# Loading the gate rows of a head pair as two broadcasts to 64 partitions each

## The chip, the cores and the metric

The kernel runs on one core of a Trainium2 chip. The metric is the device time of one execution in microseconds (us); the time of a kernel is the median of several runs. A trace of one further execution, taken by the hardware profiler, gives the rows below. The engines are PE (TensorE, matmuls; PEld its weight loads), DVE (VectorE), ACT (ScalarE), POOL (GpSimd) and SP (SyncE, which here only issues DMA transfers, in program order). The DMA transfers themselves run on 16 DMA engines.

## The reference

Three stages run one after the other on 2 x 576 tokens with 512 features:

```python
# attention with a forget gate: B, H, S, D = 2, 8, 576, 64
cum = np.cumsum(np.log(np.clip(f, 0.0001, 1.0)), axis=-1)
scores = q @ k.T / np.sqrt(D) + cum[:, :, :, None] - cum[:, :, None, :]
attn = softmax(where(causal, -1e9, scores));  x = attn @ v        # heads side by side: 1152 x 512
# mixture of 4 experts, 512 -> 1024 -> 512, weighted by p = domain_probs / sum
x = sum(p[:, e:e+1] * (np.maximum(x @ w1[e], 0) @ w2[e]) for e in range(4))
# MLP, 512 -> 2048 -> 512
h = x @ w_in;  out = (h / (1 + np.exp(-1.702 * h))) @ w_out
```

## The kernel before, in words

The tokens are four chunks (`CH`): 256 and 320 tokens of each of the two batch entries. Attention and the expert layers are interleaved: `attention()` is a generator of attention steps, and the main loop over `seq` emits expert matmuls (`emit_l1`, line 687, and `emit_l2`, line 736, twelve matmuls for each of four groups `g`) and pulls attention steps between them. Chunk 0 is done first with its order fixed by hand (`in_turn`, `first_step`). Then two passes over head pairs follow: the pass of chunk 1 (four head pairs), then that of chunks 2 and 3 (four more). Elsewhere a scheduler places the instructions of each engine.

For each head pair the kernel loads keys (`kq`) and queries (`qr`), values (`vd`), and the row of `cum` of each head, written to DRAM as `cumd` before. `load_cum` does the last: into two tiles `cb` (one for each head, the first 512 columns of its row in all 128 partitions) and one tile `cbs` (576 columns; head 0's row in partitions 0 to 63, head 1's in partitions 64 to 127, for the last 64 queries of both heads, which are worked on together). `prep_cum` on POOL adds the causal mask `tri` to the diagonal blocks: lines 404 and 407 for `cb`, line 410 for `cbs`, one small addition for each half of the tile. `emit_max` (line 475, DVE) adds `cb` or `cbs` to the scores in PSUM and takes the row maximum. ACT exponentiates (line 491), POOL normalises (line 500), PE transposes (line 518), ACT copies the result (`ph`, line 56), and PE multiplies with the values (line 548).

Expert weights come in pairs of groups into `wst` (`load_pair`, 512 KB). ACT rounds each group to `whi` (line 56), DVE takes the remainder `wlo` (line 173), and the matmuls of lines 687 and 736 use both.

All these loads are issued through `load` (line 62) on one queue, that of SP, in the order of the program. `cbs_p` has two buffers, so the load of a `cbs` waits until DVE has read the one from two head pairs before; what stands behind it on the queue waits too.

Of the kernel before, what the change touches and what calls it, by code (L numbers as in the profile page):

```python
# [15 lines left out]
B, H, S, D = 2, 8, 576, 64  # L16
# [19 lines left out]
def attn_moe_mlp(ctx: ExitStack, tc: tile.TileContext, qk0, qk1, qk2, v0, vp, fg, dp, wa_moe, wb_moe, wa_mlp, wb_mlp, outT):  # L36
# [8 lines left out]
    def pool(name, bufs, space=None, scope=ctx):  # L45
        kw = {} if space is None else {"space": space}
        return scope.enter_context(tc.tile_pool(name=name, bufs=bufs, **kw))
# [12 lines left out]
    def load(out, in_):  # L60

        ins = nc.sync.dma_start(out=out, in_=in_)
        if start[0]:
            tc.keep_in_program_order(ins)
# [37 lines left out]
    cumd = pool("cumd", 1, bass.MemoryType.DRAM).tile([16, S], F32, name="cumd")  # L102
# [284 lines left out]
    def load_cum(p, h0):  # L387

        cs, b, s0 = p
        st = pairs[p, h0]  # L390
        r = b * H + h0
        st["cb"] = [cb_p.tile([128, 896], F32, tag="cb", name="cb") for _ in range(2)]
        for g, cb in enumerate(st["cb"]):
            load(cb[:, :512], cumd[r + g:r + g + 1, :512].to_broadcast([128, 512]))
        st["cbs"] = cbs_p.tile([128, S], F32, tag="cbs", name="cbs")
        load(st["cbs"], cumd[r:r + 2, :].unsqueeze(1).to_broadcast([2, 64, S]))

    def prep_cum(p, h0):

# [185 lines left out]
    def first_step(i):  # L585
# [30 lines left out]
        if i == 0:  # L616
            load_cum(p, h0)
# [5 lines left out]
    def attention():  # L623
# [16 lines left out]
        for i in range(len(seq) + L_X2 + 1):  # L640
# [9 lines left out]
            for k in [k for k in nxt if first[k] == i + 2]:  # L650
                load_cum(*k)
# [281 lines left out]
```

## Time and profile before

| | |
|---|---|
| time, median of 3 runs | 744.79 us (743.59 to 745.51) |
| profiled execution | 746.29 us, of which 744.6 us from the first to the last instruction (the span) |
| busy in the span | PE 716.6, PEld 686.9, DVE 460.5, POOL 289.4, ACT 272.3 us |
| mean granted clock of TensorE | 0.982 of full speed |

An engine's busy time is a sum over stages. Matmuls are pipelined and their ends are modelled, so a busy PE is not a PE at its peak; where PE stands idle or runs at a lower granted clock is read from the trace by stage.

### The profile page before, as it was taken

What the parts mean: (1) busy time and instruction counts of PE and PEld (TensorE: products, weight loads), DVE (VectorE), ACT (ScalarE), POOL (GpSimd) and SP (SyncE); (2) the same over time, 40 slices, a digit from 0 to 9 for tenths busy, and PEclk for the clock granted to TensorE, in tenths of its full rate; (3) what the DMA queues carried; (4) which work ended last, traced back from release to release, by engine and by line L of the source; (5) the groups of instructions that cost most, each with busy time, mean ns of one, the idle gap of its engine ahead of it and who ended that gap; (6) DMA issues with size and microseconds to landing.
All of it is one profiled execution on the core that took longest, in us unless ns stands there. A gap on an engine that the chain in (4) does not pass through costs nothing.

```text
span 744.6 us, 12024 instructions
## 1 busy us (share of the span) xinstructions
PE 716.6 (96%) x4520; PEld 686.9 (92%) x4520; DVE 460.5 (62%) x1023; ACT 272.3 (37%) x636; POOL 289.4 (39%) x368
## 2 busy tenths in 40 slices
PE   7986888999999999999999999999999999999998
PEld 4676777888999999999999999999999999999998
DVE  6474357667667999999999833334983124424422
ACT  5444447656642232232212211222444433323420
POOL 4585577887242204223323333232352222222220
PEclk9698999999999999999999999999999999999999
DMA  8484544624215554644443401000100000000012
GB/s 241 139 269 126 173 139 151 208 90 119 86 57 192 157 181 142 183 150 128 142 142 96 105 27 57 1 1 1 57 1 0 1 1 1 1 1 0 1 44 85
DMA packets 31226, 68.83 MB, mean 92 GB/s; under 512 B 3224, under 2 KB 4768, under 8 KB 31168
## 3 DMA queue, kind: packets, MB, share of 16 engines
q1 hardware_dynamic: 31128, 68.02, 29.4%
q8 instruction: 36, 0.59, 0.3%
q14 instruction: 22, 0.18, 0.1%
q10 hardware_dynamic: 40, 0.04, 0.0%
HBM read 65.62 MB, written 2.41 MB: 91 GB/s over the span
## 4 chain that ended last, share of the span: by engine, by line
PE 76%; DVE 9%; DMA 7%; POOL 2%; issue 2%; ACT 2%; SPq 1%; POOLq 0%; ACTq 0%; DVEq 0%
PE m L736 34%; PE m L687 33%; PE x L548 3%; DMA wst<-in_wb_moe_dram 3%; DMA wst<-in_wa_moe_dram 3%; PE s L449 3%; PE t L518 3%; DVE wlo L173 2%; POOL e L500 1%; ACT e L491 1%; DVE hl L719 1%; DVE wf L228 1%; DVE cvd L234 1%; DVE tmp L750 1%; DVE cvt L222 1%
## 5 line engine op out<-in xcount | busy, mean ns | idle before, releaser
L752 POOL TENSOR_TENSOR acc<-acc,tmp 128x384 f32<-128x384 f32 (+3 forms) x112 | 111.9, 1009 | 240.1 <-DVE tmp L750 238.5
L687 PE MATMUL m<-xh,whi 128*128 128x384 f32 (+2 forms) x624 | 126.4, 322 | 11.9 <-ACT whi L56 5.5
L736 PE MATMUL m<-hh,wlo 128*128 128x384 f32 (+2 forms) x640 | 128.1, 319 | 1.3 <-DVE wlo L173 1.3
L736 PE MATMUL m<-hh,whi 128*128 128x384 f32 (+2 forms) x640 | 128.7, 320 | 0.6 <-DVE hl L714 0.5
L736 PE MATMUL m<-hl,whi 128*128 128x384 f32 (+2 forms) x640 | 127.4, 319 | 0.0
L687 PE MATMUL m<-xl,whi 128*128 128x384 f32 (+2 forms) x624 | 126.4, 322 | 0.0
L687 PE MATMUL m<-xh,wlo 128*128 128x384 f32 (+2 forms) x624 | 126.2, 322 | 0.0
L173 DVE TENSOR_TENSOR wlo<-wst,whi 128x512 fp32r<-128x512 f32 x112 | 96.3, 862 | 42.8 <-ACT whi L56 40.5
L56 ACT ACTIVATE whi<-wst 128x512 fp32r<-128x512 f32 x108 | 67.1, 628 | 138.2 <-PE m L687 62.8
L687 PEld LDWEIGHTS m<-xh,whi 128*128 128x128 f32 x624 | 104.0, 189 | 12.9 <-ACT whi L56 5.7
L736 PEld LDWEIGHTS m<-hh,wlo 128*128 128x128 f32 x640 | 106.0, 188 | 2.1 <-DVE wlo L173 1.9
L736 PEld LDWEIGHTS m<-hh,whi 128*128 128x128 f32 x640 | 106.2, 189 | 1.5 <-DVE hl L714 0.7
L736 PEld LDWEIGHTS m<-hl,whi 128*128 128x128 f32 x640 | 106.0, 189 | 0.2
L687 PEld LDWEIGHTS m<-xl,whi 128*128 128x128 f32 x624 | 104.8, 190 | 0.3
L687 PEld LDWEIGHTS m<-xh,wlo 128*128 128x128 f32 x624 | 104.6, 190 | 0.3
L727 POOL TENSOR_TENSOR hl<-tmp,hh 128x384 fp32r<-128x384 f32 x48 | 49.0, 1024 | 133.3 <-ACT hh L56 133.2
L718 ACT ACTIVATE hh<-m 128x384 fp32r<-128x384 f32 (+2 forms) x108 | 47.3, 439 | 114.4 <-PE m L687 114.4
L719 DVE SCALAR_TENSOR_TENSOR hl<-m,hh 128x384 fp32r<-128x384 f32 (+2 forms) x108 | 53.0, 494 | 33.9 <-ACT hh L718 33.8
L725 DVE TENSOR_TENSOR tmp<-m,sg 128x384 f32<-128x384 f32 x48 | 26.6, 554 | 54.2 <-ACT sg L724 54.2
L750 DVE TENSOR_TENSOR tmp<-m,dpb 128x384 f32<-128x384 f32 (+2 forms) x80 | 40.8, 511 | 30.3 <-PE m L736 27.3
L500 POOL TENSOR_SCALAR e<-e,sm 128x128 f32<-128x128 f32 (+4 forms) x72 | 44.9, 634 | 36.1 <-DVE sm L498 28.6
L491 ACT ACTIVATE e<-e,mx 128x128 f32<-128x128 f32 (+4 forms) x72 | 42.0, 583 | 29.0 <-DVE mx L475 27.5
(99 smaller groups left out, 783.3 us busy)
## 6 DMA issues: line engine op xcount, KB each, us to landing
wst<-in_wa_moe_dram SPq DMA_DIRECT2D x28, 512.0 KB, 4.2
wst<-in_wb_moe_dram SPq DMA_DIRECT2D x28, 512.0 KB, 4.4
mst<-in_wa_mlp_dram SPq DMA_DIRECT2D x16, 512.0 KB, 3.8
mst<-in_wb_mlp_dram SPq DMA_DIRECT2D x16, 512.0 KB, 3.6
cb<-cumd SPq DMA_DIRECT2D x16, 256.0 KB, 4.8
qr<-in_qk_dram SPq DMA_DIRECT2D x12, 256.0 KB, 10.7
kq<-in_qk_dram SPq DMA_DIRECT2D x8, 352.0 KB
vd<-in_vp_dram SPq DMA_DIRECT2D x8, 320.0 KB, 10.6
```

The source lines that it names most:

```text
L56: return nc.scalar.activation(out=out, in_=in_, func=AF.Copy)
L173: nc.vector.tensor_sub(lf, raw, f(hf))
L491: nc.scalar.activation(out=e[:, off:off + w], in_=e[:, off:off + w], func=AF.Exp, scale=-1.0, bias=mx, accum_out=sm[:, 0, k:k + 1])
L500: nc.gpsimd.tensor_scalar(out=e[:, off:off + w], in0=e[:, off:off + w], scalar1=sm[:, 0, i:i + 1], scalar2=1.0, op0=ALU.mult, op1=ALU.mult)
L687: nc.tensor.matmul(p[:, :n], lhsT=w[:, k, :], rhs=x[c][:, k, :], start=(j == 0 and k == 0), stop=(j == 2 and k == 3))
L718: nc.scalar.activation(out=hh[:, g, :n], in_=p[:, :n], func=AF.Relu)
L719: nc.vector.scalar_tensor_tensor(out=hl[:, g, :n], in0=p[:, :n], scalar=0.0, in1=f(hh[:, g, :n]), op0=ALU.max, op1=ALU.subtract)
L725: nc.vector.tensor_mul(t[:, :n], p[:, :n], s[:, :n])
L727: nc.gpsimd.tensor_sub(hl[:, g, :n], t[:, :n], f(hh[:, g, :n]))
L736: nc.tensor.matmul(p[:, :n], lhsT=w[:, k, :], rhs=x[:, k, :n], start=(j == 0 and k == 0), stop=(j == 2 and k == 3))
L750: nc.vector.tensor_mul(t[:, :n], p[:, :n], d)
L752: nc.gpsimd.tensor_add(a, a, t[:, z])
```

## The change

```diff
@@ load_cum
         st["cbs"] = cbs_p.tile([128, S], F32, tag="cbs", name="cbs")
-        load(st["cbs"], cumd[r:r + 2, :].unsqueeze(1).to_broadcast([2, 64, S]))
+        for g in range(2):
+            load(st["cbs"][64 * g:64 * g + 64], cumd[r + g:r + g + 1, :].to_broadcast([64, S]))
```

One transfer whose source is walked as two rows, each repeated 64 times, becomes two transfers, each of one row repeated 64 times. The bytes that are written are the same, 288 KB for a head pair, and there are eight head pairs. Line numbers above 396 are one higher in the changed kernel.

On SP's queue, in the pass of chunk 1 around the third head pair, the piece of the difference reads (names are tiles and inputs, `wst` the expert weights):

```order
 L62 DMA wst<-in_wa_moe_dram 128x2x512
 L62 DMA cb<-cumd 128x512 x2
-L62 DMA cbs<-cumd 128x1x576
+L62 DMA cbs<-cumd 64x576 x2
 L62 DMA wst<-in_wa_moe_dram 128x2x512
 L62 DMA vd<-in_vp_dram 128x640
```

Nothing else moves on this queue; at each of the eight places two transfers stand for one, ahead of the same followers.

On POOL, at the same head pair, the kernel before has (`e` are the attention weights, `khi` and `klo` the split keys of a later pair):

```order
L404 TENSOR_TENSOR cb<-cb,tri 128x128
L407 TENSOR_TENSOR cb<-cb,tri 128x128
L53 TENSOR_SCALAR khi<-kq 128x704
L500 TENSOR_SCALAR e<-e,sm 128x576
L410 TENSOR_TENSOR cbs<-cbs,tri 64x64 x2
L374 TENSOR_TENSOR klo<-kq,khi 128x704
L466 MEMSET e 128x64
L500 TENSOR_SCALAR e<-e,sm 128x384 x2
```

and the changed kernel has:

```order
L405 TENSOR_TENSOR cb<-cb,tri 128x128
L408 TENSOR_TENSOR cb<-cb,tri 128x128
L53 TENSOR_SCALAR khi<-kq 128x704
L411 TENSOR_TENSOR cbs<-cbs,tri 64x64
L501 TENSOR_SCALAR e<-e,sm 128x576
L411 TENSOR_TENSOR cbs<-cbs,tri 64x64
L374 TENSOR_TENSOR klo<-kq,khi 128x704
L501 TENSOR_SCALAR e<-e,sm 128x384 x2
L467 MEMSET e 128x64
```

The addition to the first half of `cbs` now stands ahead of the normalisation of `e`, that to the second half behind it. PE, DVE and ACT keep their instructions up to swaps of neighbours in the two passes, and nothing moves behind the attention.

## Rows read from the trace of the kernel before

**Rows 1.** The chain that ended last, its largest shares by line.

```profile
PE m L736 34%; PE m L687 33%; PE x L548 3%; DMA wst<-in_wb_moe_dram 3%; DMA wst<-in_wa_moe_dram 3%; PE s L449 3%; PE t L518 3%; DVE wlo L173 2%; POOL e L500 1%; ACT e L491 1%; DVE hl L719 1%; DVE wf L228 1%; DVE cvd L234 1%; DVE tmp L750 1%; DVE cvt L222 1%
```

**Rows 2.** Busy time by stretch: the pass of chunk 1, then of chunks 2 and 3.

```profile
core 0: us, PE busy (x) PEld busy (x) DVE busy (x) ACT busy (x) POOL busy (x), PEclk, DMA share, GB/s
40.00:120.00 80.00, 62.35 (x430) 55.47 (x429) 45.28 (x128) 37.81 (x99) 55.30 (x87) 0.91 0.51 153
120.00:216.00 96.00, 95.07 (x700) 86.26 (x698) 67.24 (x218) 62.05 (x170) 65.64 (x97) 1.00 0.43 130
```

**Rows 3.** The chain between 38 and 130 us: start, us, what.

```profile
40.48 12.62 DMA wst<-in_wb_moe_dram
...
60.96 10.27 DMA wst<-in_wa_moe_dram
...
101.04 10.12 DMA wst<-in_wb_moe_dram
```

**Rows 4.** PE in order of time, where it stood over 2 us [idle before].

```profile
55.08 0.74 PE L687 MATMUL m<-xh,whi 128*128 128x256 f32 x4 [2.04 <-DVE acc L747]
...
72.00 1.22 PE L687 MATMUL m<-xh,whi 128*128 128x256 f32 x4 [5.48 <-ACT whi L56]
...
94.67 3.96 PE L548 MATMUL x<-ph,vd 128*64 128x320 f32 x20 [4.28 <-ACT ph L56]
...
114.19 0.74 PE L687 MATMUL m<-xh,whi 128*128 128x256 f32 x4 [4.36 <-DVE hl L719]
```

**Rows 5.** SP's queue in order of time at the third head pair.

```profile
60.37 0.51 SPq L62 DMA_DIRECT2D cbs<-cumd  x1
60.96 0.42 SPq L62 DMA_DIRECT2D wst<-in_wa_moe_dram  x1
```

**Rows 6.** Busy time by stretch around two of the four stalls (columns as in rows 2).

```profile
62.00:64.00 2.00, 2.00 (x16) 1.86 (x15) 1.16 (x6) 0.87 (x4) 2.00 (x4) 1.00 0.90 162
64.00:66.00 2.00, 2.00 (x17) 1.86 (x16) 0.00 (x0) 0.00 (x0) 0.26 (x1) 1.00 1.01 336
...
70.00:72.00 2.00, 0.00 (x1) 0.00 (x1) 0.02 (x1) 0.69 (x2) 1.74 (x3) 0.64 0.13 52
72.00:74.00 2.00, 1.44 (x5) 1.15 (x6) 2.00 (x4) 2.00 (x6) 0.66 (x2) 0.50 0.09 35
...
110.00:112.00 2.00, 0.00 (x0) 0.00 (x0) 0.15 (x1) 0.82 (x2) 1.72 (x3) 1.00 0.13 51
```

**Rows 7.** Waits of POOL, 40 to 120 us (us, times, longest), largest.

```profile
POOL cbs L410 <- DMA cbs<-cumd: 15.9, 4, 6.0
```

**Rows 8.** POOL in order of time at the third head pair.

```profile
70.10 0.70 POOL L410 TENSOR_TENSOR cbs<-cbs,tri 64x64 f32<-64x64 f32 x2 [5.85 <-DMA cbs<-cumd]
```

**Rows 9.** DMA issues: count, KB each, median us from issue to landing.

```profile
wst<-in_wa_moe_dram SPq DMA_DIRECT2D x28, 512.0 KB, 4.2
...
dpb<-dpT SPq DMA_DIRECT2D x2, 288.0 KB, 4.4
```

**Rows 10.** A stretch at the start, loads of 64 partitions in flight (columns as rows 2).

```profile
3.00:4.00 1.00, 1.00 (x4) 0.35 (x3) 0.88 (x3) 0.67 (x2) 0.97 (x5) 1.00 0.73 213
```

**Rows 11.** The chain: PE's pieces behind two stalls, and like pieces later.

```profile
73.78 1.09 PE s L449 x3
74.86 1.71 PE m L687 x8
76.57 2.62 PE x L548 x20
...
114.19 2.36 PE m L687 x12
...
116.76 3.00 PE x L548 x20
...
130.82 2.21 PE x L548 x20
...
138.82 0.40 PE s L449 x3
...
229.04 1.44 PE m L687 x12
```

## The prediction, made before the changed kernel ran

> **What bounds the kernel now.** I read the chain that ended last first. Matmuls hold most of it, but two DMA entries stand high in it, the loads of expert weights `wst`, with 3% each [rows 1]. A transfer belongs there only while an engine stands and waits for it, so the next view was busy time by stretch: in the pass of chunk 1, 40 to 120 us, PE is busy for 62.35 of 80 us at a mean clock of 0.91, in the pass after it for 95.07 of 96 us at 1.00 [rows 2]. The loss lies in the first of the two. There the chain runs through four loads of `wst`; three are shown, of 12.62, 10.27 and 10.12 us (the fourth, between the last two, is like them) [rows 3], where the median load of `wst` lands after 4.2 us [rows 9]. PE in order of time shows what that costs: four stalls of 2.04, 5.48, 4.28 and 4.36 us, 16.16 us together, each released by something made from the weights that came late or queued behind it on ACT or DVE [rows 4].
>
> Why are these loads late? On SP's queue the load of `cbs` stands just ahead of `wst`, 60.37 and 60.96 us [rows 5]. `cbs` lands at 70.10 us, 9.7 us after its issue (POOL, which had waited 5.85 us for it, starts then) [rows 8], and `wst` 1.1 us behind it, at 60.96 + 10.27 = 71.23. The load of `dpb`, as large (288 KB, a row repeated over 128 partitions), takes 4.4 us [rows 9]. What differs shows in the share of the DMA engines: from 62 to 66 us it is 0.90 to 1.01, but in the last two microseconds ahead of the landing, 70 to 72, it is 0.13 at 52 GB/s, and at the last stall again 0.13 at 51 GB/s [rows 6]. 0.13 of 16 engines is two engines. So I read the old `cbs` as carried by two engines, 147 KB on each, while the other fourteen go ahead and run dry; `wst` has a share on those two as well, behind `cbs`, and isn't complete before that.
>
> **The change part by part.**
>
> *Issue.* One more transfer for each of eight head pairs, 0.5 us of SP's queue each [rows 5]. Where the queue is waited for, `wst` is issued 0.5 us later; that is in the estimate below. Elsewhere it is hidden by the span of what SP waits for anyway.
>
> *Landing.* No row shows a row broadcast to 64 partitions. The nearest from above is the old load, 9.7 us; from below the broadcast of 288 KB to 128 partitions, 4.4 us. Loads of 64 partitions at the start keep 0.73 of the 16 engines busy [rows 10], so 64 partitions do not confine a transfer to a few. I take about 5 us for both halves, near the lower end.
>
> *The weights behind it.* If the two halves lie evenly on 16 engines, `wst` has 295 KB more ahead of it on all of them: 0.9 us at the 336 GB/s of [rows 6]. I estimate 4.2 + 0.9 us from its issue, which is 0.5 us later: 60.96 + 0.5 + 5.1 = 66.6 in place of 71.23, that is 4.7 us earlier. PE stood from 66.5 (72.00 less 5.48) and restarted 0.8 us behind the landing, so about 0.8 us of this stall stays. At the last stall 101.04 + 5.6 = 106.6 in place of 111.16, 4.5 us earlier against a stall of 4.36; the third is like it. The first, 2.04 us, had its load landing at 53.10; the same two engines hold it, so it goes too. Gain: 16.16 - 0.8 = 15.4 us.
>
> *The clock.* [...] Against like pieces at full clock [rows 11]: behind the second stall 1.09 for 0.40, 1.71 for 0.96 (eight at 1.44 / 12) and 2.62 for 2.21, 1.85 us more; behind the third 3.96 [rows 4] for 2.21, 1.75; behind the fourth 2.36 for 1.44 and 3.00 for 2.21, 1.71. Together 5.3 us, which go where the stalls go. The stall of 2.04 us has no such slow pieces behind it (0.74 for four, not 1.22) [rows 4], so the 0.8 us that stay should cost no clock.
>
> *POOL.* Its waits for `cbs` in the first pass, 15.9 us in four [rows 7], fall to some 3 us: it came to the addition 3.9 us after the issue at the third head pair, so with a landing of 5 to 5.5 us it still waits 1 to 1.5 us, and about as long at the next. This is no further gain but a limit: POOL is busy for 55.30 of the 80 us [rows 2]. PE's stretch would shrink to 80 - 15.4 - 5.3 = 59.3 us. POOL needs 55.3 + 3 = 58.3 if none of its other waits (80 - 55.3 - 15.9 = 8.8 us) remain, and 67 if all do. Both engines would be nearly full, and where they wait for each other time is lost; I take 2 us off.
>
> *Second pass.* PE is idle for 0.93 of its 96 us [rows 2]: 0.8 us is what an earlier `cbs` can bring at most, and I take it. After the attention nothing moves, and what follows starts earlier by as much.
>
> Sum: 15.4 + 5.3 - 2.0 + 0.8 = 19.5 us. The profiled execution took 746.29 us, 1.5 us more than the median shown; 746.3 - 19.5 = 726.8, and for a median 744.8 - 19.5 = 725.3 us.
>
> [...] The trace shows two engines at work at the end of each such burst [rows 6], so the halves are not a mere splitting of one even transfer. [...]
>
> **The rivals.** *POOL sets the pace of the first pass.* If its other waits of 8.8 us stay, the pass takes 67 us and the gain is 13 + 0.8, 731 us. For it: it would then be busy for over 80% of the pass. Against it: in the second pass PE hardly stands with POOL busy for 65.64 of 96, and part of the 8.8 us came behind the late weights.
>
> *The transfers of a burst share the engines without order,* and `wst` is complete only with the last of its burst. In the second burst 2.03 MB are issued together; 0.32 and 0.67 MB have moved by 66 us [rows 6], the rest takes 3.1 us at 336 GB/s, so `wst` would land at 69.1, 2.1 us earlier than now. Four times that is 8.4 us with the clock hardly mended: 736 us. Against it: `cbs` and `wst` landed 1.1 us apart in the order of issue.
>
> *The halves are not spread,* each lands as late as the whole: 744.8 us, within 0.3%, which is about what a measurement of this kernel can tell from no change. [rows 10] speak against it.
>
> *Slower: POOL's new order.* The first half's addition now stands ahead of a normalisation of `e`. If that half landed as late as now, the normalisation would wait up to 5.85 us, and PE's transposes behind it; since PE stood there later anyway, I price it at 2 us, and with 0.5 us of issue ahead of each of four late loads at 4 us: 749 us. It decides only if landing stays near 9 us; under some 5 us POOL hardly waits.
>
> **How the numbers follow.** The forecast as worked out (720 to 730): 0.62. POOL's pace (730 to 735): 0.20. Burst without order: 0.08. Not spread: 0.05. Slower: 0.03. More than 25 us gained: 0.02. The predicted time is the first, 725.3; 720 to 735 holds 0.82. Faster by over 0.3%: 0.62 + 0.20 + 0.08 + 0.02 = 0.92; within: 0.05; slower: 0.03.
>
> **What would show it.** Right: no stretch of the first pass with the DMA share at 0.13; loads of `wst` out of the chain there, or at 4 to 6 us; PE's four stalls gone but for a microsecond, the clock at 1.00 through the pass; POOL's waits for `cbs` at a few microseconds; the span of the first pass near 61 us and all that follows unchanged in length. Wrong: the share of 0.13 still there (not spread); no tail, but `wst` at 8 us (no order); or stalls of PE released by POOL's normalisation (POOL's pace).

## The result, and the profile after

The changed kernel takes 726.04 us (median of 4 runs, 722.93 to 727.28), the kernel before 744.19 us beside it (4 runs, 743.25 to 745.51): ratio 0.9749, 95% interval 0.9719 to 0.9778. In a second comparison on another occasion it was 724.44 against 746.5 us, ratio 0.971 (0.9676 to 0.9743). So the gain is 18 to 22 us. The profiled execution of the changed kernel was its quickest, 722.93 us, and that of before lies 2.1 us above its median; the two traces therefore differ by 23.4 us, more than the medians do.

Where did the time go from? I cut both traces at the same work. The first mark is the first matmul of line 736 (737 after), chunk 0's second expert layer; the second is the end of the third of chunk 1's four products with the values (line 548, 549 after). All four late loads of weights land between them, and this stretch is called the first pass here; the fourth product lies behind the mark, among the work of the second pass. Busy time by stretch, after:

```profile
core 0: us, PE busy (x) PEld busy (x) DVE busy (x) ACT busy (x) POOL busy (x), PEclk, DMA share, GB/s
39.40:99.20 59.80, 56.87 (x428) 50.89 (x429) 45.74 (x128) 37.51 (x96) 55.36 (x84) 1.00 0.58 201
...
99.19:232.96 133.77, 133.77 (x993) 124.94 (x994) 97.32 (x272) 73.20 (x196) 74.53 (x107) 1.00 0.44 140
```

and the same work before ([rows 2] cut it at round numbers):

```profile
40.70:119.80 79.10, 61.52 (x422) 54.84 (x423) 44.84 (x128) 36.95 (x97) 54.46 (x85) 0.91 0.51 152
...
119.76:256.13 136.37, 135.44 (x999) 125.62 (x1000) 97.11 (x272) 73.61 (x196) 75.05 (x106) 1.00 0.45 138
```

The first pass is 19.3 us shorter; the second, cut at the start of a block of 48 matmuls behind the attention (the third mark), 2.6. Of these 21.9 us, 15.6 are idle time of PE (17.58 + 0.93 before, 2.93 + 0 after), and 6.3 are busy time (196.96 against 190.64), at a clock of 1.00 in place of 0.91 in the first pass. The next 1.3 us lie ahead of the first mark (39.4 for 40.7); they are put down to the execution and not to the change, since a kernel that has the old loads up to there (the last experiment but one, below) also came to this mark at 39.48. What follows the third mark takes 488.2 us, before 488.5.

What answers to the chain of [rows 1], its shares by line, and to [rows 3], the one load of `wst` that is left in it in the first pass: the two loads of 3% are gone from the upper places, one is left with 1%.

```profile
PE m L688 38%; PE m L737 37%; PE s L450 3%; PE x L549 3%; PE t L519 3%; POOL e L501 1%; PE m L786 1%; DMA qr<-in_qk_dram 1%; DVE wlo L173 1%; POOL qlo L385 1%; DMA wst<-in_wa_moe_dram 1%; POOL acc L753 1%; DVE cvt L220 1%; POOL cb L408 0%; DVE tmp L751 0%
```

```profile
71.95 4.31 DMA wst<-in_wa_moe_dram
```

PE's waits between 39 and 100 us (us in total, times, longest), where [rows 4] had four stalls of 16.16 us together:

```profile
PE t L519 <- POOL e L501: 1.1, 2, 0.8
PE m L688 <- DVE hl L720: 1.0, 1, 1.0
PE m L737 <- DVE hl L715: 0.5, 1, 0.5
PE s L450 <- DVE mx L476: 0.3, 1, 0.3
```

SP's queue at the third head pair, then POOL in order of time there; they answer to [rows 5] and [rows 8]:

```profile
55.24 1.09 SPq L62 DMA_DIRECT2D cbs<-cumd  x2
56.43 0.54 SPq L62 DMA_DIRECT2D wst<-in_wa_moe_dram  x1
```

```profile
60.72 0.32 POOL L411 TENSOR_TENSOR cbs<-cbs,tri 64x64 f32<-64x64 f32 x1
61.02 0.74 POOL L501 TENSOR_SCALAR e<-e,sm 128x576 f32<-128x576 f32 x1
61.85 0.32 POOL L411 TENSOR_TENSOR cbs<-cbs,tri 64x64 f32<-64x64 f32 x1
```

Neither addition carries a bracket: when POOL comes to them, both halves are there. Before, POOL stood 5.85 us at this place. The same burst by stretch, which answers to [rows 6]:

```profile
60.00:62.00 2.00, 2.00 (x18) 1.95 (x17) 0.70 (x2) 0.26 (x1) 1.92 (x4) 1.00 1.01 390
62.00:64.00 2.00, 2.00 (x16) 1.86 (x16) 1.09 (x1) 1.75 (x5) 1.88 (x2) 1.00 1.03 387
64.00:66.00 2.00, 2.00 (x16) 1.75 (x15) 1.97 (x6) 2.00 (x8) 0.42 (x1) 1.00 0.28 104
```

No stretch of 0.13 with PE standing beside it is left; the engines work together at up to 390 GB/s and are done, and PE is busy throughout at full clock. The DMA issues (count, KB each, median us to landing) show that not only the weights waited. After:

```profile
wst<-in_wa_moe_dram SPq DMA_DIRECT2D x28, 512.0 KB, 4.3
...
qr<-in_qk_dram SPq DMA_DIRECT2D x12, 256.0 KB, 6.1
vd<-in_vp_dram SPq DMA_DIRECT2D x8, 320.0 KB, 4.9
cbs<-cumd SPq DMA_DIRECT2D x16, 144.0 KB, 5.2
```

Before, `qr` took 10.7 and `vd` 10.6 us, also behind `cbs` on the queue. The median of `wst` hardly moves (4.2 before), because only a few of its loads stood behind a `cbs`: a median over a whole kernel hides four late ones.

### The profile page after: what moved, and what is told of

Read it like the earlier page. It is cut to its first block, busy times and chain, and to the rows that moved or that the text cites. A ratio compares the mean times of both kernels' runs of the same rounds, so it can differ in the third digit from the quotient of the medians.

```text
span 721.2 us, 12050 instructions
## 1 busy us (share of the span) xinstructions
PE 707.9 (98%) x4520; PEld 680.3 (94%) x4520; DVE 462.0 (64%) x1023; ACT 272.5 (38%) x636; POOL 289.8 (40%) x368
## 4 chain that ended last, share of the span: by engine, by line
PE 86%; DVE 5%; POOL 5%; DMA 2%; issue 1%; ACT 1%; POOLq 0%; DVEq 0%; ACTq 0%
PE m L688 38%; PE m L737 37%; PE s L450 3%; PE x L549 3%; PE t L519 3%; POOL e L501 1%; PE m L786 1%; DMA qr<-in_qk_dram 1%; DVE wlo L173 1%; POOL qlo L385 1%; DMA wst<-in_wa_moe_dram 1%; POOL acc L753 1%; DVE cvt L220 1%; POOL cb L408 0%; DVE tmp L751 0%
## 5 line engine op out<-in xcount | busy, mean ns | idle before, releaser
L501 POOL TENSOR_SCALAR e<-e,sm 128x128 f32<-128x128 f32 (+4 forms) x72 | 47.9, 674 | 36.6 <-DVE sm L499 26.6
```

The lines of the kernel that those rows point to most:

```text
L501: nc.gpsimd.tensor_scalar(out=e[:, off:off + w], in0=e[:, off:off + w], scalar1=sm[:, 0, i:i + 1], scalar2=1.0, op0=ALU.mult, op1=ALU.mult)
```

## The experiments

The theory: the old source, walked as two rows, puts the transfer on two engines; the weights behind it have a share on these two and are complete only after it. Rivals: the number of engines doesn't matter, but the two smaller transfers do; the loss is POOL's wait for the gate rows and not the weights; the transfer is costly wherever it is queued.

### How many engines

The halves stay as in the change, and so does every engine's order of instructions. Only the source of each half is walked as 2, 4 or 8 repeats, with 32, 16 or 8 copies each (the edit for 2 is shown).

```diff
-            load(st["cbs"][64 * g:64 * g + 64], cumd[r + g:r + g + 1, :].to_broadcast([64, S]))
+            load(st["cbs"][64 * g:64 * g + 64], cumd[r + g:r + g + 1, :].unsqueeze(1).to_broadcast([2, 32, S]))
```

> Each half is walked as a source of 2 by 32 repeats of its row in place of 64; the order of the instructions on every engine is that of the changed kernel, still two transfers. Theory (the old load lay on two DMA engines, and the weights behind it waited for those two): both halves lie on two engines again, 147 KB on each, the DMA share of 0.13 at the end of each burst comes back, wst lands some 10 us after its issue, PE's four stalls return, 742 to 748 us. Rival (the gain comes from two transfers in place of one, or from the order that the scheduler made of them): 724 to 728 us, as the changed kernel.

> As the run with 2 by 32, but 4 by 16 repeats. Theory: four engines with 74 KB each, so at the pace of the old load (147 KB in some 7.7 us) about 3.9 us, wst some 3 us later than in the changed kernel and the share at the end of a burst 0.25; stalls of PE of 2 to 3.5 us at three places, with little loss of clock: 731 to 739 us. Rival: 724 to 728 us.

> As before with 8 by 8 repeats. Theory: eight engines with 37 KB each, about 1.9 us, wst 1 us later than in the changed kernel, which PE sees little of: 726 to 730 us. Rival: 724 to 728 us.

Measured on one chip, where the kernel before took 747.25 us: with 2 repeats 754.55 us, ratio 1.0106 (1.0083 to 1.0129); with 4, 731.9 us, 0.98 (0.9762 to 0.9839); with 8, 729.11 us, 0.9763 (0.9746 to 0.978). The change itself (64) stands at 0.9749 and 0.971. The split in two transfers, the bytes and the order are the same in all four, so the gain hangs on the number of repeats in the slowest dimension of the source: two lose it, four have most of it. Four and eight came out in their expected ranges, two did not. The chain of the kernel with 2 repeats has the four late weights again, later than in [rows 3]:

```profile
39.83 12.91 DMA wst<-in_wb_moe_dram
...
61.01 11.75 DMA wst<-in_wa_moe_dram
...
83.97 11.42 DMA wst<-in_wa_moe_dram
...
105.90 11.58 DMA wst<-in_wb_moe_dram
```

and at their end the old tail, at half clock:

```profile
72.00:74.00 2.00, 0.48 (x2) 0.48 (x3) 0.50 (x1) 1.16 (x3) 1.92 (x2) 0.50 0.13 51
```

With 4 repeats the stretch behind the issue of the gate rows, ahead of the burst of the weights, shows about twice that share, and PE goes on:

```profile
60.00:62.00 2.00, 2.00 (x18) 1.92 (x17) 1.25 (x6) 0.46 (x1) 0.88 (x2) 1.00 0.27 73
```

0.13 of 16 engines is about two, 0.27 about four: in these two stretches as many as the source has repeats in its slowest dimension. For eight and 64 repeats no row shows such a number; the order of the times (754.55, 731.9, 729.11 us) fits it.

The kernel with 2 repeats came out 6.6 us above its expected range and slower than before. Three things differ from before there: the split in two transfers, POOL's order, and that both engines now read the same row. The next run takes away the last. The two halves keep two as their slowest dimension, but each walks both rows, so that half of the partitions hold the other head's row. That this leaves them on two engines is an estimate from the 0.13 above; the share was not read here.

```diff
-            load(st["cbs"][64 * g:64 * g + 64], cumd[r + g:r + g + 1, :].to_broadcast([64, S]))
+            load(st["cbs"][64 * g:64 * g + 64], cumd[r:r + 2, :].unsqueeze(1).to_broadcast([2, 32, S]))
```

> As the run with halves of 2 by 32 repeats, but each half is made of both heads' rows, 32 times each, so its two engines read two different rows at a time as the old load did; half of the partitions hold the other head's row. That run was 7 us slower than the kernel before, with wst 11.4 to 11.8 us after its issue. If two engines reading one row slow each other, wst lands after 10.2 us again and some 4 us come back: 747 to 751 us beside a kernel before of 747. If the excess is only POOL's new order (the first half ahead of the normalisation), the time stays at 752 to 756.

752.39 us, ratio 1.0052 (1.0029 to 1.0075), and weights after 13.03, 10.30, 11.08 and 10.90 us. The time lies at the lower edge of the range for POOL's order. By the ratios, taken on two chips and with intervals that just miss each other, up to about half of the excess goes with reading one row from both engines. The rest is left for the split and POOL's new order, which no run here separates; that the order has a part is seen in the traces: in both kernels PE stands for POOL's normalisation of `e`, 2.6 us with one row and 1.7 with two, which POOL gets to only after the first half has landed:

```profile
67.14 0.31 POOL L411 TENSOR_TENSOR cbs<-cbs,tri 64x64 f32<-64x64 f32 x1 [4.11 <-DMA cbs<-cumd]
67.44 0.74 POOL L501 TENSOR_SCALAR e<-e,sm 128x576 f32<-128x576 f32 x1
71.94 0.32 POOL L411 TENSOR_TENSOR cbs<-cbs,tri 64x64 f32<-64x64 f32 x1 [3.77 <-DMA cbs<-cumd]
```

(from the kernel with 2 repeats of one row).

### One transfer in place of two

One row to all 128 partitions, in one transfer; head 1's row is left out, and head 0's stands in its place.

```diff
-        for g in range(2):
-            load(st["cbs"][64 * g:64 * g + 64], cumd[r + g:r + g + 1, :].to_broadcast([64, S]))
+        load(st["cbs"], cumd[r:r + 1, :].to_broadcast([128, S]))
```

> One transfer as in the kernel before, but of one row broadcast to all 128 partitions: head 0's row stands for head 1's as well. Theory: one transfer of the same 288 KB over 16 engines does what two do, no share of 0.13, no long stalls, 723 to 728 us. Rival (two transfers with two completions are what helps): 742 to 746 us.

727.57 us, ratio 0.9744 (0.9723 to 0.9765), `cbs` landing after 5.0 us in the median. The second transfer's issue and smaller size make no difference that can be measured, though the scheduler's order of the engines' instructions differs in places from both kernels. So two transfers bring nothing against one that lands after 5.0 us, as in this run (0.9744 against 0.9749 and 0.971); against the old one, 9.7 us at the third head pair [rows 8], they bring the 18 to 22 us.

### The weights, or POOL's wait

The changed kernel gets one more transfer of 288 KB at each head pair, into DRAM that nobody reads, between the halves and the weights: once with the old source (two rows), once as a control with one row to 128. The two have the same bytes and the same order, which is not quite that of the changed kernel, so they are compared with each other; only the weights and what follows stand behind the extra transfer, the gate rows don't.

```diff
+    extra_p = pool("extra", 2, bass.MemoryType.DRAM)
...
+        load(extra_p.tile([2, 64, S], F32, tag="extra", name="extra"), cumd[r:r + 2, :].unsqueeze(1).to_broadcast([2, 64, S]))
```

```diff
+        load(extra_p.tile([128, S], F32, tag="extra", name="extra"), cumd[r:r + 1, :].to_broadcast([128, S]))
```

> The changed kernel with one more transfer behind the two halves of each head pair, ahead of wst: the old form (two rows, each 64 times, 288 KB) into a scratch in DRAM that nothing reads. The halves land early, so POOL has nothing to wait for; only what stands behind on the queue is late. Theory (nearly all of the gain was the weights behind the two engines): wst lands some 10 us after its issue, PE's stalls and the slow clock are back, 740 to 750 us. Rival (POOL's waits for cbs, 25 us of them, made the loss): 725 to 731 us.

> The control to the run with the extra transfer in the old form: the same bytes as one row broadcast to 128 rows of the scratch, same order on every engine. Theory: 1 us more ahead of wst on all engines, 726 to 731 us. Rival (the bytes themselves and one more issue are what costs): the time of that run.

The kernel before took 747.62 us on this chip. With the two-row extra 743.82 us, ratio 0.9951 (0.9932 to 0.9969); with the control 727.99 us, 0.9733 (0.9711 to 0.9755); both lie in the ranges of the theory. The difference, 15.8 us, is the price of holding what stands behind the transfer, with POOL's wait for the gate rows left out: POOL waits 0.3 us for `cbs` in this pass where it waited 15.9 [rows 7]. It stands 6.5 us for `qr`, which is held as well (1.2 in the control), but PE's three long stalls there, 5.86, 3.66 and 3.20 us, end with `whi` and `ph` on ACT, behind the weights. From 743.82 to 747.62 there are 3.8 us, which are left for POOL's wait and all else, the other order too. The chain of the first of the two has three of the four late loads again (in the control the loads behind the extra transfer take 6.30 and 6.58 us at the first and last of these places),

```profile
58.54 9.80 DMA wst<-in_wa_moe_dram
...
79.36 9.85 DMA wst<-in_wa_moe_dram
...
99.61 9.76 DMA wst<-in_wb_moe_dram
```

and its burst the old tail, with PE standing for 5.86 us and the clock at half:

```profile
64.00:66.00 2.00, 0.00 (x0) 0.00 (x0) 0.00 (x0) 0.00 (x0) 0.30 (x2) 0.93 1.04 376
66.00:68.00 2.00, 0.00 (x0) 0.00 (x0) 0.00 (x0) 0.00 (x0) 0.00 (x0) 0.50 0.32 124
68.00:70.00 2.00, 0.96 (x4) 0.96 (x5) 0.98 (x2) 1.64 (x5) 0.00 (x0) 0.50 0.13 51
```

```profile
69.04 2.07 PE L690 MATMUL m<-xh,whi 128*128 128x256 f32 x8 [5.86 <-ACT whi L56]
```

A transfer whose data nobody waits for holds the kernel up nearly as much as the old one did: 15.8 us of the 18 to 22.

### The old transfer on another queue

If the weights are held because they stand behind the old load on SP's queue, that load on ACT's queue should free them.

```diff
-        load(st["cbs"], cumd[r:r + 2, :].unsqueeze(1).to_broadcast([2, 64, S]))
+        nc.scalar.dma_start(out=st["cbs"], in_=cumd[r:r + 2, :].unsqueeze(1).to_broadcast([2, 64, S]))
```

> The kernel before with the old cbs load issued from ACT in place of SP, so wst is on another queue. Theory: cbs lands as late as before and POOL waits for it as before, but wst no longer stands behind it; if the two engines serve both queues in turn, wst lands some 6 us after its issue and the long stalls of PE shrink: 728 to 738 us. Rival (POOL's waits make the loss, or the two engines finish cbs first whatever the queue): 742 to 750 us.

759.03 us, ratio 1.015 (1.0127 to 1.0173): the expectation missed. The trace says why: the first two loads are now issued at 10.26 us, in chunk 0, among its loads, and POOL stands for the first of them:

```profile
35.08 0.70 POOL L410 TENSOR_TENSOR cbs<-cbs,tri 64x64 f32<-64x64 f32 x2 [16.89 <-DMA cbs<-cumd]
```

PE's transposes behind it wait 14.25 us, and chunk 0 ends some 15 us later. So this kernel tells little of the first pass, and another followed, in which the first two head pairs stay on SP's queue:

```diff
+        old = cumd[r:r + 2, :].unsqueeze(1).to_broadcast([2, 64, S])
+        if p == passes[1] and h0 <= 2:
+            load(st["cbs"], old)
+        else:
+            nc.scalar.dma_start(out=st["cbs"], in_=old)
```

> The kernel before, but from the third head pair on its gate rows (still one transfer with two source rows) are loaded from ScalarE's queue, so that the first two pairs stand on SyncE's queue as before. Theory (the loss is the weights that stand behind the gate rows on SyncE's queue): the stage weights land in about 4 to 5 us, the gate rows as late as before, GpSimd waits 2 to 3 us for each; the first stall of 2.04 us stays; 727 to 733 us. Rival (the loss is the transfer itself, two engines carrying 288 KB, wherever it is queued): 742 us or more.

The kernel before took 746.5 us on this chip, this one 742.54 us, ratio 0.9949 (0.9927 to 0.9971). By its time the rival has it; by its trace each theory has a part. The first pass ran from 39.48 to 106.47 us, 67.0 us, 12.1 shorter than before and 7.2 longer than in the changed kernel: late weights are mostly gone from it. But the second pass, from there to the block of 48 matmuls at 250.93, takes 144.5 us, 8.1 longer than before. Three rows show it (ACT's queue, POOL, PE in order of time):

```profile
110.99 0.51 ACTq L400 DMA_DIRECT2D cbs<-cumd  x1
```

```profile
125.16 1.25 POOL L414 TENSOR_TENSOR cbs<-cbs,tri 64x64 f32<-64x64 f32 x2 [8.95 <-DMA cbs<-cumd]
```

```profile
132.88 0.69 PE L522 MATMUL t<-identr,e 128*128 128x128 f32 x2 [7.62 <-POOL e L504]
```

The load lands 14.2 us after its issue, beside a burst on SP's queue, and POOL's four pieces of `e` wait behind the addition, so PE does too. The first kernel with ACT's queue has the same place (POOL 8.42, PE 7.0 us). So here the second queue did not cure the old transfer: most of the wait moved from the weights to the gate rows. The order has a part in that which these runs leave open: the scheduler moved instructions on every engine in both kernels, and in the kernel before two of those four pieces of `e` stand ahead of the addition.

The changed kernel itself ran beside it, to have both on one chip.

> The changed kernel itself, unedited, on the chip of the run beside it: 723 to 728 us. The difference of the two is the price of late gate rows when no weights stand behind them: 4 us by the pair of runs with the extra transfers, 7 at most; a rival by which late gate rows cost nothing gives 0 to 1.

724.44 us, as expected. The difference to the run above, 18.1 us, is no price of POOL's late rows alone, as I had meant it, because the first head pairs there stay on SP's queue and the second pass got a wait that the kernel before hasn't.

## Why the prediction was right

The forecast was 725.3 us; 726.04 and 724.44 us were measured. The mechanism held, but a hit within 1 us is in part luck: the two comparisons differ by 4 us in the gain, and between the marks of the two traces 21.9 us went, where the sum had 19.5.

*Two engines hold the old transfer.* Shown by runs that change the number of repeats alone (ratios 1.0106, 0.98, 0.9763), and by the extra transfer, which brings back late weights, stalls, clock and the share of 0.13.

*Landing and weights.* About 5 us for the halves: the median is 5.2. `wst` was put at 5.1 us from its issue and 0.5 us later in the queue; the one load of the first pass that stands in the chain took 4.31 us, and `wst` follows 1.19 us behind the first `cbs`, not 0.59, 0.6 later. The allowance of 0.9 us for the bytes ahead went by 336 GB/s; the burst now runs at 390. That the halves would lie evenly on 16 engines was my estimate from [rows 10], and no row shows it for them alone: from 57 to 58 us, behind their issue, the share is 0.59, in the burst 1.01 to 1.03.

*Stalls.* Predicted 15.4, and 0.8 in the second pass, less 2.0 where PE and POOL hold each other up: 14.2 us. PE's idle time fell by 15.6. Of the 2.93 us left in the first pass, 1.1 are released by POOL.

*Clock.* Predicted 5.3. In the first pass, where the clock was 0.91 and is 1.00, PE's busy time fell by 4.65 us (61.52 to 56.87) with six more matmuls in it (428 for 422); at about 0.12 us each (1.44 for 12 [rows 11]) that is some 5.4 us for the same work. Matmul ends are modelled, so a part of a microsecond here stays open. One sign of the prediction does not hold: that the first stall costs no clock was read from its first four pieces (0.74 us), but those behind the fourth stall took 0.74 us too [rows 4], and there the clock fell a microsecond later. The granted clock itself bears the reading out (before, behind the first stall and behind the fourth):

```profile
55.00:56.00 1.00, 0.93 (x7) 0.93 (x8) 1.00 (x4) 0.33 (x2) 0.73 (x1) 1.00 0.14 53
...
115.00:116.00 1.00, 1.00 (x7) 1.00 (x6) 1.00 (x2) 0.98 (x5) 1.00 (x2) 0.50 0.00 0
```

*POOL.* The step that failed in its mechanism. I let POOL wait some 3 us for the halves; it waits for none. I had taken its arrival at the addition, 3.9 us behind the issue, from before; now it comes 5.5 us behind it (55.24 to 60.72), busy with other work till then, and the halves are there. The 8.8 us of its other waits fell as well: POOL is busy for 55.36 of 59.80 us, so that 4.4 us of idle time are left. The allowance of 2 us came out near enough for another reason than its working.

*Second pass.* Predicted 0.8, measured 2.6. The idle part is 0.93, as bounded; the other 1.7 us are busy time. Both traces have 1421 matmuls in the two passes together (422 + 999 before, 428 + 993 after), so six moved ahead of the mark between them, some 0.7 us. The transposes behind the mark, 119 in both, keep PE busy for 19.40 us before and 18.85 after; the last 0.4 us stay open.

*The rivals.* POOL's pace: its other waits fell to half, and PE waited for it 1.1 us. No order in a burst: the full share is reached and `wst` is there after 4.31 us. Not spread: excluded by the landing of 5.2 us. Slower by POOL's new order: not here, but the mechanism is real under the condition that was put to it. With the halves as late as the whole, 752.39 against 747.62 us were measured, the split included, and PE standing for `e` behind the first half; 4 us had been priced.

## What to carry to other kernels

Where a load lands late, look at the share of the DMA engines in the last microseconds ahead of it: a small constant share (0.13, two of 16) was here the sign of a transfer ahead in the queue that lies on a few engines, and `wst` behind it came 10.1 to 12.6 us after its issue, and 9.8 us behind a transfer whose data nobody needed. What helped was a source whose slowest dimension is longer, one row to 64 partitions in place of two rows to 64 each (ratio 0.9749, with the price of a second transfer in it); moving it to another queue cost 11 us in one kernel here and won 4 in the other. And see what the late data holds up in program order on the engine that uses it: with an addition put one place earlier PE stood 2.6 and 1.7 us for the normalisation behind it, where before no such wait was over 0.8.

## What was not expected of the hardware

Halves walked as two repeats of one row seem slower than halves walked as both rows, though by the estimate above both lie on two engines: weights behind them landed after 11.75, 11.42 and 11.58 us against 10.30, 11.08 and 10.90 (the three loads behind the first; that one took 12.91 and 13.03), and the kernels took 754.55 and 752.39 us on different chips, ratios 1.0106 and 1.0052. With one trace each and ratios that are barely apart, this is not more than likely, and why is open. And the change hardly needs its 64 repeats: with four, at a share of 0.27 behind the issue, the ratio is 0.98, with eight 0.9763, against 0.9749 and 0.971.
